# Retention with chunk products on halves of the tensor engine, one state sum per chunk, and a decay table from eight scans

## The chip, the cores and the metric

The kernel runs on one core of a Trainium2 chip. The metric is the device time of one execution in microseconds; lower is better. Times are medians of several executions; profiles come from one profiled execution.

## The reference

Three layers follow one another. Only the first, a retention (linear attention with a decay per head), is touched:

```python
# q, k, v: [B=2, H=8, S=768, D=64]; lam: [8]; block = 64
rel = pos[:, None] - pos[None, :]
Dmask = np.where(rel >= 0, lam[:, None, None] ** rel[None, :, :], 0.0)
lam_pow = lam[:, None, None] ** (pos[None, :, None] + 1)
lam_block = lam ** block
for b in range(nb):
    qb, kb, vb = q[:, :, sl], k[:, :, sl], v[:, :, sl]
    intra = np.einsum('bhic,bhjc->bhij', qb, kb) * Dmask[None]
    intra = np.einsum('bhij,bhjd->bhid', intra, vb)
    inter = np.einsum('bhid,bhde->bhie', qb * lam_pow[None], kv_state)
    out[:, :, sl] = intra + inter
    rev_pow = lam[:, None, None] ** (block - 1 - pos[None, :, None])
    kv_state = lam_block * kv_state + np.einsum('bhsd,bhse->bhde', kb * rev_pow, vb)
```

The result is the same for any block length. Behind it stand a layer norm with a two-layer network (512 to 2048 to 512, ReLU, residual) on 1,536 tokens, and an attention of four experts (64 wide) of which the two best by a gate are summed for each token.

## The kernel before

The retention runs over 12 chunks of 128 tokens (2 batches of 6), each with its own loads of `qkT` and `kv` (three buffers each). Inside a chunk it works with blocks of C = 64 tokens: the partitions hold two of them, LATE (partitions 0 to 63, since keys and values are stored backwards) and EARLY. All products of the retention are 64x64 in fp32 on a quarter of TensorE's array; each appears in the profile as two matmul passes with a weight load each.

For chunk n the loop at L647 does this:

- `ret_scores(n + 1)` (L328): 16 products of keys and queries into `sck`.
- `ret_state(n)` (L358): 16 products of decayed keys `kd` and values, one 64x64 state per head and block, into the other half of the same PSUM tile.
- `ret_inner(n)` (L391): 16 products of values and the decayed scores `a`, into a PSUM tile `po`.
- `ret_sum(n, EARLY)` (L370): VectorE adds the first block's state to the carried one (`st`, L379); it also waits for the inner products. GpSimd multiplies it by the decay of 64 tokens (`old`, L389).
- `ret_decay(n + 1)` (L346): decayed keys `kd` for three heads on ScalarE (L351) and five on GpSimd (L352), scores times decay table `a` on VectorE (L355).
- Steps of the layer norm of finished blocks of 384 tokens (`ln_a` to `ln_d`), as they come due.
- `room(early)`: side work on VectorE and ScalarE, taken from a list by costs in us until the room is used up. The list holds the norm's pieces and the decoding of the first weights of the network (`prep_parts`, 6 pieces for each of 4 weights in front of the end of the retention).
- `ret_sum(n, LATE)`: the second block's state sum, and `old` again.
- From chunk 5 on, if one is ready, one step of the network's first layer (`g1`, L504, 12 matmuls of 128x384); before chunk 5 three matmuls on zeros (`warm`).
- `ret_outer(n)` (L406): up to 16 products of states and scaled queries `qd`, added into `po`; `ret_qd(n + 1)` on GpSimd (L340).
- `leave()`, VectorE's and ScalarE's end of the expert step; `ret_copy(n)`: ScalarE copies `po` to `xT` (L423); a second `room`.

Two PSUM tiles of two banks (`ps_big`) carry `sck` and `po` in turn. The order on every engine's queue is the order of the program, written by hand. Only between the start (`begin`, closed at L290) and L637 does a planner place what stands on VectorE, ScalarE, GpSimd and the DMA queue.

At the start the decay table `dec` (128 x 8 x 64) comes from one scan over 512 elements on VectorE (L284), which needs two prepared tables: `mul` (lam, zero at the start of each head) and `one` (from `hit`, made by GpSimd). GpSimd makes the powers `qpow` by doubling (L298) and all constants of later layers (L303 to L315), and issues the load of `g_ln`.

After the last chunk the steps of the network follow (L691, then `mlp_step`).

Of the kernel before, what the change touches and what calls it, by code (L numbers as in the profile page):

```python
# [17 lines left out]
P = 128  # L18
# [11 lines left out]
C = 64  # L30
# [6 lines left out]

ROOM = ((0.7, 0.9), (1.4, 1.6))
# [31 lines left out]
def model(ctx, tc, qkT, kv, lam, g_ln, w12, wat, out):  # L70
# [191 lines left out]
    qpow = rc.tile([P, HP, C], F32, tag="qpow", name="qpow")  # L262
    lq = rc.tile([P, H], F32, tag="lq", name="lq")
    dec = rc.tile([P, H, C], F32, tag="dec", name="dec")
    mul = rc.tile([P, H, C], F32, tag="mul", name="mul")
    one = rc.tile([P, H, C], F32, tag="one", name="one")
    hit = rc.tile([P, C], F32, tag="hit", name="hit")
    order = [(b, c) for b in range(B) for c in range(NC)]
    begin = ExitStack()
    begin.enter_context(tc.manual_schedule(engines={  # L270
        mybir.EngineType.SP, mybir.EngineType.DVE, mybir.EngineType.Activation, mybir.EngineType.Pool}))
    nc.sync.dma_start(lq, lam.rearrange("h o -> o h").to_broadcast([P, H]))
    ret_load(*order[0])
    table = const.tile([P, 1], F32, tag="table", name="table")
# [44 lines left out]

    LATE, EARLY = 0, 1
    SCK, ST = {}, {}

    def half(a2):
        return ts(a2 * C, (a2 + 1) * C)

    def ret_scores(n):  # L328

# [676 lines left out]
```

## Time and profile before

| | us |
|---|---|
| median of 3 runs | 489.55 (487.71 to 490.32) |
| the profiled execution | 488.7 |
| its span, first to last instruction | 486.8 |
| TensorE matmul busy | 465.2 (96%), 4,219 instructions |
| VectorE busy | 337.4 (69%) |
| ScalarE busy | 198.0 (41%) |
| GpSimd busy | 99.4 (20%) |
| mean granted clock of TensorE | 0.993 |

The page gives busy time by engine, 40 slices of the span with the busy share of each engine, the granted clock and the DMA, the chain that ended last, and the costliest groups. PE is the matmul side of TensorE and PEld its weight loads, DVE is VectorE, ACT ScalarE, POOL GpSimd, SP the engine that issues most DMAs. PE's busy time counts a matmul from its start to its modelled end, so passes overlap: distances between starts tell more than durations. A wait stands with the engine that waited, the line it then ran, and what released it ("issue": nothing that the profile shows).

### The profile page before, as it was taken

Reading aid. Unit: us, or ns where it says so; the run is one execution under the profiler, and the core shown is the slowest. Engines: PE = TensorE matmul, PEld = TensorE weight load, DVE = VectorE, ACT = ScalarE, POOL = GpSimd, SP = SyncE. Lnnn points to the kernel's source line nnn. Section 1 sums busy time; section 2 is a strip of 40 time slices with the busy share of each in tenths; the row PEclk is TensorE's granted clock in tenths of the full one; section 3 lists DMA queues with packets and bytes.
Section 4 is the critical chain, followed back from the end, with each engine's and each line's share of the span. In section 5 each row is a group of like instructions: output and inputs, shape, how many; then the busy total and the mean of one; then the engine's idle time right before and its main releaser. Section 6 shows DMA issues by size and latency. Waiting matters only on the chain.

```text
span 486.8 us, 10377 instructions
## 1 busy us (share of the span) xinstructions
PE 465.2 (96%) x4219; PEld 432.4 (89%) x4224; DVE 337.4 (69%) x715; ACT 198.0 (41%) x453; POOL 99.4 (20%) x149
## 2 busy tenths in 40 slices
PE   7577989999999999999999999999999999999996
PEld 4456767999999999999999999999998889898884
DVE  2658795797999976942899935255478686676663
ACT  2337645532224331311233502122256666548672
POOL 6566452000000000000000000000045534334340
PEclk9979999999999999999999999999999999999999
DMA  8768520121232312210222400000000000000111
GB/s 286 298 205 294 179 92 3 43 88 44 87 131 86 114 60 88 87 44 1 86 88 86 131 0 2 0 1 1 0 2 0 24 23 22 24 3 23 44 43 67
DMA packets 10735, 35.28 MB, mean 72 GB/s; under 512 B 1344, under 2 KB 1600, under 8 KB 10688
## 3 DMA queue, kind: packets, MB, share of 16 engines
q1 hardware_dynamic: 10512, 34.49, 20.5%
q8 instruction: 33, 0.54, 0.5%
q10 hardware_dynamic: 144, 0.13, 0.1%
q14 instruction: 14, 0.11, 0.1%
q0 software_dynamic: 32, 0.00, 0.0%
HBM read 31.47 MB, written 3.15 MB: 71 GB/s over the span
## 4 chain that ended last, share of the span: by engine, by line
PE 84%; DVE 7%; ACT 3%; issue 3%; POOL 1%; DMA 1%; DVEq 0%; POOLq 0%; ACTq 0%
PE h L513 26%; PE y L547 26%; PE pj L764 4%; PE s L844 4%; PE av L893 4%; PE o L914 4%; PE t L881 4%; PE pv L786 3%; PE yf L566 2%; PE po L416 2%; PE sck L366 1%; PE po L399 1%; PE sck L336 1%; ACT xn L455 1%; PE warmc L106 1%
## 5 line engine op out<-in xcount | busy, mean ns | idle before, releaser
L513 PE MATMUL h<-xn,w 128*128 128x384 f32 x768 | 140.5, 337 | 0.0
L513 PEld LDWEIGHTS h<-xn,w 128*128 128x128 f32 x768 | 133.3, 188 | 2.7 <-issue 1.2
L547 PE MATMUL y<-hs,w 128*128 128x384 f32 x552 | 99.8, 334 | 0.0
L547 PEld LDWEIGHTS y<-hs,w 128*128 128x128 f32 x552 | 96.1, 188 | 0.0
L778 POOL TENSOR_SCALAR kh<-kh 64x384 fp32r<-64x384 f32 x16 | 8.4, 523 | 291.4 <-DVE qs L772 280.0
L532 ACT ACTIVATE hs<-h 128x384 fp32r<-128x384 f32 x50 | 24.5, 490 | 103.5 <-PE h L513 90.0
L533 DVE SCALAR_TENSOR_TENSOR hs<-h,hs 128x384 fp32r<-128x384 f32 x50 | 27.7, 555 | 42.5 <-ACT hs L532 42.5
L552 DVE TENSOR_TENSOR xT<-xT,y 128x768 f32<-128x768 f32 x30 | 28.5, 950 | 31.6 <-PE y L547 31.6
L871 POOL TENSOR_SCALAR att<-att,c,gw 128x128 f32<-128x128 f32 (+5 forms) x48 | 35.8, 752 | 52.0 <-DVE c L868 16.3
L231 ACT CAST w<-top 128x512 fp32r<-128x512 f32 x32 | 19.9, 621 | 48.0 <-DVE top L225 46.3
L764 PE MATMUL pj<-x,wa 128*128 128x384 f32 x192 | 35.0, 337 | 0.0
L764 PEld LDWEIGHTS pj<-x,wa 128*128 128x128 f32 x192 | 33.4, 188 | 0.0
L882 ACT COPY aT<-t 128x512 f32<-128x512 f32 (+3 forms) x64 | 26.6, 441 | 11.0 <-PE t L881 10.6
L881 PE MATMUL t<-ident,att 128*128 128x128 f32 x168 | 26.2, 275 | 0.3 <-DVE qs L772 0.3
L243 DVE TENSOR_TENSOR w<-top,mag 128x512 fp32r<-128x512 f32 x32 | 24.3, 758 | 0.3
L216 ACT ACTIVATE mag<-raw 128x512 f32<-128x512 f32 x32 | 21.2, 668 | 7.0 <-DVE w L243 7.0
L236 DVE SCALAR_TENSOR_TENSOR mag<-raw,mag 128x512 f32<-128x512 uint32 x32 | 23.3, 727 | 0.6
L893 PE MATMUL av<-aT,v 128*64 128x128 f32 x336 | 23.6, 280 | 0.0
L844 PE MATMUL s<-kh,qs 128*128 128x512 f32 (+3 forms) x64 | 23.3, 365 | 0.0
L225 DVE SCALAR_TENSOR_TENSOR top<-raw,mag 128x512 int32<-128x512 int32 x32 | 22.1, 689 | 0.5
L240 DVE TENSOR_TENSOR top<-top,w 128x512 f32<-128x512 f32 x32 | 22.4, 699 | 0.0
L893 PEld LDWEIGHTS av<-aT,v 128*64 128x64 f32 x336 | 17.8, 136 | 4.4 <-issue 3.9
(132 smaller groups left out, 735.9 us busy)
## 6 DMA issues: line engine op xcount, KB each, us to landing
raw<-in_w SPq DMA_DIRECT2D x32, 512.0 KB, 3.5
qk<-in_qkT SPq DMA_DIRECT2D x12, 512.0 KB, 5.2
kvn<-in_kv SPq DMA_DIRECT2D x12, 512.0 KB, 6.0
out<-os SPq DMA_DIRECT2D x11, 256.0 KB, 2.0
rawa<-in_wat SPq DMA_DIRECT2D x3, 512.0 KB, 3.2
rawa<-in_wat SPq DMA_DIRECT2D x1, 520.0 KB, 3.9
out<-os SPq DMA_DIRECT2D x1, 128.0 KB, 1.7
out<-os ACTq DMA_DIRECT2D x1, 128.0 KB, 1.7
```

The lines of the kernel that those rows point to most:

```text
L243: nc.vector.tensor_tensor(t["w"][:, 1], t["top"], t["mag"], ALU.add)
L513: nc.tensor.matmul(ph[:, :TB], w[:, wi, k, :], xn[:, xi, k, :], start=(i == 0), stop=(i == 11))
L532: LAST.append((nc.scalar.activation(h[:, 0], ph[:, :TB], AF.Relu), nc.vector.scalar_tensor_tensor(h[:, 1], ph[:, :TB], 0.0, h[:, 0].bitcas ...
L533: nc.vector.scalar_tensor_tensor(h[:, 1], ph[:, :TB], 0.0, h[:, 0].bitcast(F32), ALU.max, ALU.subtract)))
L547: nc.tensor.matmul(y[:, j, :TB], w[:, wi, e * P:(e + 1) * P], h[:, xi], start=(f == 0 and i == 0), stop=(f == GF - 1 and i == 2))
L552: nc.vector.tensor_tensor(xv, xv, y[:, :, :TB], ALU.add)
L764: nc.tensor.matmul(ps[:, :TB], w[:, wi, k, :], x2[:, xi, k, :], start=(i == 0), stop=(i == 11))
L844: nc.tensor.matmul(ps[:, c0:c1], q, kk[:, e, c0:c1], start=(i == 0), stop=(i == 1))
L871: nc.gpsimd.tensor_scalar(a[:, :n], a[:, :n], c, gw, ALU.mult, ALU.mult)
L881: nc.tensor.transpose(pt[:, (j - j0) * P:(j - j0 + 1) * P], a[:, j * P:(j + 1) * P], ident)
L882: nc.scalar.copy(aT[:, j0 * P:j1 * P], pt[:, :(j1 - j0) * P])
L893: nc.tensor.matmul(pav[e2 * HD:(e2 + 1) * HD, pr * P:(pr + 1) * P], v[:, j, e * HD:(e + 1) * HD], row["aT"][e][:, j * P:(j + 1) * P], star ...
```

## The change

The block becomes the chunk: 128 tokens. Scores are 8 products with 64 rows and 128 columns of the array and 128 moving columns; the state is one per head and chunk, 8 products over 128 rows; inner products are 8 over 128 rows with 128 moving columns; the cross-chunk products are 8 of 64x64 with 128 moving columns, and none in a batch's first chunk. One state sum and one `old` remain for each chunk, without the wait for the inner products, and none in a batch's last chunk (`old` not in the last two). State and output share one `po` tile, `sck` holds scores alone. The order in a chunk is scores(n + 1), state, cross-chunk, inner; then decay(n + 1), sum, `qd`(n + 1), copy; then norm steps, the network's step or `warm`, one `room` of 1.5 us (3.0 with a step), and the step's `leave`.

`dec` is 128 x 8 x 128 and comes from eight scans of 128 elements that read lam as a broadcast column, so `one` and `mul` go. `qpow` doubles once more. The constants of later layers are issued on GpSimd behind chunk 0's decayed keys, `g_ln` is loaded through ScalarE's queue ahead of its table load, and the whole start is in the order of the program. Of the products' functions (L322 to L423) the diff below shows the new form alone.

```diff
-ROOM = ((0.7, 0.9), (1.4, 1.6))
+ROOM = (1.5, 3.0)
...
-    qpow = rc.tile([P, HP, C], F32, tag="qpow", name="qpow")
+    qpow = rc.tile([P, HP, P], F32, tag="qpow", name="qpow")
     lq = rc.tile([P, H], F32, tag="lq", name="lq")
-    dec = rc.tile([P, H, C], F32, tag="dec", name="dec")
-    mul = rc.tile([P, H, C], F32, tag="mul", name="mul")
-    one = rc.tile([P, H, C], F32, tag="one", name="one")
-    hit = rc.tile([P, C], F32, tag="hit", name="hit")
+    dec = rc.tile([P, H, P], F32, tag="dec", name="dec")
+    hit = rc.tile([P, P], F32, tag="hit", name="hit")
     order = [(b, c) for b in range(B) for c in range(NC)]
-    begin = ExitStack()
-    begin.enter_context(tc.manual_schedule(engines={
+    by_hand = ExitStack()
+    by_hand.enter_context(tc.manual_schedule(engines={
         mybir.EngineType.SP, mybir.EngineType.DVE, mybir.EngineType.Activation, mybir.EngineType.Pool}))
     nc.sync.dma_start(lq, lam.rearrange("h o -> o h").to_broadcast([P, H]))
     ret_load(*order[0])
+    g_sb = const.tile([P, KT], F32, tag="g", name="g_sb")
+    nc.scalar.dma_start(g_sb, g_ln)
     table = const.tile([P, 1], F32, tag="table", name="table")
     nc.scalar.copy(table, zeros[:, :1])
     nc.gpsimd.memset(hit, 0.0)
-    for a2 in range(2):
-        nc.gpsimd.affine_select(hit, hit, [[1, C]], ALU.not_equal, 1.0, base=1 - C * (a2 + 1), channel_multiplier=1)
-    nc.vector.tensor_copy(one, hit[:, None, :].to_broadcast([P, H, C]))
-    nc.vector.tensor_copy(mul, lq[:, :, None].to_broadcast([P, H, C]))
-    nc.vector.memset(mul[:, :, 0:1], 0.0)
-    nc.vector.tensor_tensor_scan(dec.rearrange("p h i -> p (h i)"), mul.rearrange("p h i -> p (h i)"),
-                                 one.rearrange("p h i -> p (h i)"), 0.0, ALU.mult, ALU.add)
+    nc.gpsimd.affine_select(hit, hit, [[1, P]], ALU.not_equal, 1.0, base=1 - P, channel_multiplier=1)
+    for h in range(H):
+        nc.vector.tensor_tensor_scan(dec[:, h, :], lq[:, h:h + 1].to_broadcast([P, P]), hit, 0.0, ALU.mult, ALU.add)
     ret_load(*order[1])
     load_next()
     ret_load(*order[2])
     load_next(2)
-    begin.close()
-    g_sb = const.tile([P, KT], F32, tag="g", name="g_sb")
-    nc.gpsimd.dma_start(g_sb, g_ln)
     for h2 in range(2):
         nc.gpsimd.tensor_copy(qpow[h2 * D:(h2 + 1) * D, :, 0:1], lq[h2 * D:(h2 + 1) * D, h2 * HP:(h2 + 1) * HP, None])
     m = 1
-    while m < C:
+    while m < P:
         nc.gpsimd.tensor_tensor(qpow[:, :, m:2 * m], qpow[:, :, :m],
                                 qpow[:, :, m - 1:m].to_broadcast([P, HP, m]), ALU.mult)
         m *= 2
     sum_w = const.tile([P, 32], F32, tag="sumw", name="sum_w")
-    nc.gpsimd.memset(sum_w, 1.0 / DM)
     part_w = const.tile([P, P], F32, tag="partw", name="part_w")
-    nc.gpsimd.memset(part_w, 1.0 / 32)
     eps_sb = const.tile([P, 1], F32, tag="eps", name="eps_sb")
-    nc.gpsimd.memset(eps_sb, LN_EPS)
     ident = const.tile([P, P], F32, tag="ident", name="ident")
-    make_identity(nc, ident)
     tri = const.tile([P, P], I32, tag="tri", name="tri")
     fill = const.tile([P, P], F32, tag="fill", name="fill")
-    nc.gpsimd.memset(fill, 0.0)
-    nc.gpsimd.affine_select(fill, fill, [[-1, P]], ALU.is_ge, 1.0, base=0, channel_multiplier=1)
-    nc.gpsimd.tensor_copy(tri, fill)
-    nc.gpsimd.memset(fill, MASKED)
+    def constants():
+        nc.gpsimd.memset(sum_w, 1.0 / DM)
+        nc.gpsimd.memset(part_w, 1.0 / 32)
+        nc.gpsimd.memset(eps_sb, LN_EPS)
+        make_identity(nc, ident)
+        nc.gpsimd.memset(fill, 0.0)
+        nc.gpsimd.affine_select(fill, fill, [[-1, P]], ALU.is_ge, 1.0, base=0, channel_multiplier=1)
+        nc.gpsimd.tensor_copy(tri, fill)
+        nc.gpsimd.memset(fill, MASKED)
...
+    ST = {}
+    HEADS = [(hp, h2) for hp in range(HP) for h2 in range(2)]
+    def half(h2):
+        return ts(h2 * D, (h2 + 1) * D)
+    def cols(hp, n=P):
+        return ts(hp * n, (hp + 1) * n)
     def ret_scores(n):
+        r = R[order[n]]
+        sc = r["sc"] = ps_big(f"sc{n}")
+        for hp, h2 in HEADS:
+            nc.tensor.matmul(sc[:, h2, cols(hp)], r["qk"][half(h2), 1, hp, :], r["qk"][half(h2), 0, hp, :],
+                             start=True, stop=True)
+    def ret_qd(n):
+        b, c = order[n]
+        if c > 0:
+            r = R[b, c]
+            r["qd"] = r2.tile([P, HP, P], F32, tag="qd", name=f"qd{n}")
+            nc.gpsimd.tensor_tensor(r["qd"], r["qk"][:, 0], qpow, ALU.mult)
+    def ret_decay(n):
         b, c = order[n]
         r = R[b, c]
+        if c < NC - 1:
+            kvn = r["kvn"]
+            kd = r["kd"] = r2.tile([P, H, D], F32, tag="kd", name=f"kd{n}")
+            for h in range(3):
+                nc.scalar.mul(kd[:, h, :], kvn[:, 0, h, :], dec[:, h, P - 1:P])
+            nc.gpsimd.tensor_tensor(kd[:, 3:, :], kvn[:, 0, 3:, :],
+                                    dec[:, 3:, P - 1:P].to_broadcast([P, H - 3, D]), ALU.mult)
+        a = r["a"] = r2.tile([P, 2, HP, P], F32, tag="a", name=f"a{n}")
+        nc.vector.tensor_mul(a, r["sc"].rearrange("p h (k i) -> p h k i", k=HP),
+                             dec.rearrange("p (h k) i -> p h k i", h=2))
+    def ret_state(n):
         b, c = order[n]
+        r = R[b, c]
+        po = r["po"] = ps_big(f"po{n}")
+        if c < NC - 1:
+            for hp, h2 in HEADS:
+                nc.tensor.matmul(po[half(h2), 1, cols(hp, D)], r["kd"][:, h2 * HP + hp, :],
+                                 r["kvn"][:, 1, h2 * HP + hp, :], start=True, stop=True, skip_group_check=True)
+    def ret_outer(n):
+        b, c = order[n]
+        r = R[b, c]
+        if c > 0:
+            st = ST.pop(n - 1)
+            for hp, h2 in HEADS:
+                nc.tensor.matmul(r["po"][half(h2), 0, cols(hp)], st[half(h2), hp, :], r["qd"][half(h2), hp, :],
+                                 start=(hp == 0), stop=False, skip_group_check=True)
     def ret_inner(n):
         b, c = order[n]
         r = R[b, c]
+        for hp, h2 in HEADS:
+            nc.tensor.matmul(r["po"][half(h2), 0, cols(hp)], r["kvn"][:, 1, h2 * HP + hp, :], r["a"][:, h2, hp, :],
+                             start=(c == 0), stop=True, skip_group_check=True)
+    def ret_sum(n):
         b, c = order[n]
+        if c == NC - 1:
+            return
+        st = ST[n] = r2.tile([P, HP, D], F32, tag="st", name=f"st{n}")
+        pv = R[b, c]["po"][:, 1, :HP * D].rearrange("p (h e) -> p h e", h=HP)
+        if c == 0:
+            nc.vector.tensor_copy(st, pv)
+        else:
+            nc.vector.tensor_tensor(st, pv, ST["old"], ALU.add)
+        if c < NC - 2:
+            ST["old"] = r2.tile([P, HP, D], F32, tag="old", name=f"old{n}", bufs=1)
+            nc.gpsimd.tensor_tensor(ST["old"], st, qpow[:, :, P - 1:P].to_broadcast([P, HP, D]), ALU.mult)
+    def ret_copy(n):
+        b, c = order[n]
+        r = R.pop((b, c))
         t0 = b * S + c * P
+        nc.scalar.copy(xT[:, :, t0:t0 + P], r["po"][:, 0].rearrange("p (k i) -> p k i", k=KT))
...
-    SCK[0] = ps_big("sck0")
     ret_scores(0)
     warm(WARM[1], "b")
-    ret_decay(*order[0])
-    ret_qd(*order[0])
+    ret_decay(0)
+    constants()
     norm_at, n = [0] * NBLK, 0
     while n < len(order) or min(norm_at) < 4 or norm_parts or weight_parts:
         if n < len(order):
             if n + 3 < len(order):
                 ret_load(*order[n + 3])
-            SCK[n + 1] = ps_big(f"sck{n + 1}")
-            if n > 0:
+            if n + 1 < len(order):
                 ret_scores(n + 1)
             ret_state(n)
+            ret_outer(n)
             ret_inner(n)
-            if n == 0:
-                ret_scores(n + 1)
-            ret_sum(n, EARLY)
             if n + 1 < len(order):
-                ret_decay(*order[n + 1])
+                ret_decay(n + 1)
+            ret_sum(n)
+            if n + 1 < len(order):
+                ret_qd(n + 1)
+            ret_copy(n)
...
-            leave, early = None, ROOM[0]
-            if n >= MLP_FROM and any(ready(k, True) for k in range(len(FIRST) - len(steps) + len(todo))):
-                early = ROOM[1]
+            leave = next_step(True) if n >= MLP_FROM else None
+            if n < MLP_FROM:
+                warm(3, f"c{n}")
             if n > 0:
-                room(early[0])
-            ret_sum(n, LATE)
-            if early is ROOM[1]:
-                leave = next_step(True)
-            elif n < MLP_FROM:
-                warm(3, f"c{n}")
-            ret_outer(n)
-            if n + 1 < len(order):
-                ret_qd(*order[n + 1])
+                room(ROOM[leave is not None])
             if leave:
                 leave()
-            ret_copy(n)
-            if n > 0:
-                room(early[1])
```

## Rows read from the trace of the kernel before

**Rows 1.** Windows: busy us (xcount) of PE, PEld, DVE, ACT, POOL; then clock, DMA share, GB/s.

```profile
0.00:10.00 10.00, 7.33 (x75) 3.36 (x79) 3.16 (x6) 2.90 (x8) 7.61 (x27) 1.00 0.76 264
...
0.00:82.00 82.00, 65.05 (x1623) 49.19 (x1632) 54.28 (x92) 38.70 (x89) 46.52 (x69) 0.96 0.57 201
...
82.00:372.00 290.00, 289.93 (x1726) 287.65 (x1724) 207.16 (x399) 89.52 (x180) 8.68 (x16) 1.00 0.16 53
```

**Rows 2.** Windows: from chunk 0's to chunk 6's cross-chunk products, and on to chunk 11's end.

```profile
13.35:45.51 32.16, 23.63 (x763) 17.77 (x766) 20.04 (x35) 14.07 (x35) 19.66 (x22) 0.89 0.72 253
45.51:81.23 35.72, 30.31 (x716) 25.75 (x716) 29.92 (x50) 20.92 (x45) 18.12 (x20) 1.00 0.35 122
sum 67.88, PE 53.94 PEld 43.52 DVE 49.96 ACT 34.99 POOL 37.77; mean PE 26.97 PEld 21.76 DVE 24.98 ACT 17.49 POOL 18.89
```

**Rows 3.** Timeline of PE around chunk 9: start, us, instructions, idle before.

```profile
62.16 0.69 PE L336 MATMUL sck<-qk 64*64 64x64 f32 x32 [1.40 <-issue]
62.65 0.68 PE L366 MATMUL sck<-kvn,kd 64*64 64x64 f32 x32
63.11 0.68 PE L399 MATMUL po<-a,kvn 64*64 64x64 f32 x32
63.72 0.85 PE L433 MATMUL va<-dq,sum_w 128*32 128x384 f32 x8
...
67.43 1.15 PE L416 MATMUL po<-qd,st 64*64 64x64 f32 x32
```

**Rows 4.** Timeline of PE in the attention at the end (tiles of 128x64).

```profile
380.10 0.66 PE L893 MATMUL av<-aT,v 128*64 128x128 f32 x8
```

**Rows 5.** Waits of PE, 13 to 82 us: total us, times, longest.

```profile
PE sck L366 <- issue: 7.5, 5, 2.4
PE sck L336 <- issue: 1.4, 1, 1.4
PE sck L336 <- DVE st L379: 1.0, 1, 1.0
PE po L399 <- ACT xT L423: 0.9, 1, 0.9
PE sck L336 <- PE po L416: 0.8, 1, 0.8
PE po L416 <- DVE st L379: 0.7, 1, 0.7
PE sck L336 <- ACT xT L423: 0.7, 1, 0.7
```

**Rows 6.** Timeline of PE, 20 to 32.5 us: the longest stall, a product at half clock.

```profile
22.85 0.28 PE L366 MATMUL sck<-kvn,kd 64*64 64x64 f32 x3 [2.35 <-issue]
...
31.12 1.51 PE L433 MATMUL mu<-xT,sum_w 128*32 128x384 f32 x8
```

**Rows 7.** DMA by queue (packets, MB, share): stretches 0 to 82, then 20.3 to 23.

```profile
q8 instruction: 13, 0.21, 1.1%
...
q8 instruction: 1, 0.02, 2.5%
```

**Rows 8.** Groups by line (busy us, mean ns), to 82 us; then one of the page.

```profile
L355 DVE TENSOR_TENSOR a<-sck,dec 128x512 f32<-128x512 f32 x12 | 8.2, 681 | 0.1
...
L552 DVE TENSOR_TENSOR xT<-xT,y 128x768 f32<-128x768 f32 x30 | 28.5, 950 | 31.6 <-PE y L547 31.6
```

**Rows 9.** Timeline of the start: powers, decay scan, keys of chunks 0 and 1.

```profile
3.54 0.43 POOL L295 COPY qpow<-lq 64x4 f32<-64x4 f32 x2 [1.21 <-DMA lq<-in_lam]
...
5.70 1.22 DVE L284 TENSOR_TENSOR_SCAN dec<-mul,one 128x512 f32<-128x512 f32 x1
...
8.42 0.73 POOL L352 TENSOR_TENSOR kd<-kvn,dec 128x320 f32<-128x320 f32 x1
...
13.17 0.73 POOL L352 TENSOR_TENSOR kd<-kvn,dec 128x320 f32<-128x320 f32 x1
```

**Rows 10.** Windows right behind the retention.

```profile
sum 28.00, PE 28.00 PEld 26.24 DVE 22.70 ACT 13.09 POOL 0.00; mean PE 9.33 PEld 8.75 DVE 7.57 ACT 4.36 POOL 0.00
```

More of the change, by code (lines that the diff above doesn't have):

```diff
@@ L29 @@
 GF = 4
-C = 64
 H_BUFS = 5
@@ L313, in model @@
-    nc.gpsimd.affine_select(fill, fill, [[-1, P]], ALU.is_ge, 1.0, base=0, channel_multiplier=1)
-    nc.gpsimd.tensor_copy(tri, fill)
-    nc.gpsimd.memset(fill, MASKED)
-    xT = xpool.tile([P, KT, B * S], F32, tag="xT", name="xT")
[L322 to L326, printed above, removed]
-    def ret_scores(n):
-        if n < len(order):
-            r = R[order[n]]
-            qk, r["sc"] = r["qk"], SCK[n]
-            for hp in range(HP):
-                for h2 in range(2):
-                    for a2 in (LATE, EARLY):
-                        nc.tensor.matmul(r["sc"][half(a2), h2, hp * C:(hp + 1) * C], qk[half(h2), 1, hp, half(a2)],
-                                         qk[half(h2), 0, hp, half(1 - a2)], start=True, stop=True,
-                                         skip_group_check=True)
@@ L360, in ret_state @@
         r = R[b, c]
-        kvn, kd, ps = r["kvn"], r["kd"], SCK[n + 1]
-        halves = (EARLY,) if c == NC - 1 else (LATE, EARLY)
-        for hp in range(HP):
-            for h2 in range(2):
-                for a2 in halves:
-                    nc.tensor.matmul(ps[half(h2), a2, (HP + hp) * C:(HP + hp + 1) * C],
-                                     kd[half(a2), h2 * HP + hp, :], kvn[half(a2), 1, h2 * HP + hp, :],
-                                     start=True, stop=True, skip_group_check=True)
-    def ret_sum(n, a2):
-        b, c = order[n]
-        ps = SCK[n + 1]
-        if a2 == EARLY or c < NC - 1:
-            st = r2.tile([P, HP, D], F32, tag=f"st{a2}", name=f"st{b}{c}{a2}")
-            pv = ps[:, a2, HP * C:].rearrange("p (h e) -> p h e", h=HP)
-            if c == 0 and a2 == EARLY:
-                ins = nc.vector.tensor_copy(st, pv)
-            else:
-                ins = nc.vector.tensor_tensor(st, pv, ST["old"], ALU.add)
-            if a2 == EARLY:
-                for done in R[b, c]["inner"]:
-                    tc.add_manual_dep(ins.ins, done.ins.name, mybir.DependencyInfo(
-                        mybir.DependencyClass.Sync, mybir.DependencyReason.DATA), reason="rows")
-            ST[n, a2] = st
-            if c < NC - 1:
-                ST["old"] = r2.tile([P, HP, D], F32, tag="old", name=f"old{b}{c}{a2}")
-                nc.gpsimd.tensor_tensor(ST["old"], st, qpow[:, :, C - 1:C].to_broadcast([P, HP, D]), ALU.mult)
+        po = r["po"] = ps_big(f"po{n}")
[4 more added lines that the diff above has]
+    def ret_outer(n):
+        b, c = order[n]
+        r = R[b, c]
[4 more added lines that the diff above has]
+                                 start=(hp == 0), stop=False, skip_group_check=True)
     def ret_inner(n):
@@ L393, in ret_inner @@
         r = R[b, c]
-        po = r["po"] = ps_big(f"po{b}{c}")
-        r["inner"] = []
-        for hp in range(HP):
-            for h2 in range(2):
-                for a2 in (LATE, EARLY):
-                    mm = nc.tensor.matmul(
-                        po[half(h2), 1 - a2, hp * C:(hp + 1) * C], r["kvn"][half(a2), 1, h2 * HP + hp, :],
-                        r["a"][half(a2), h2, hp, :], start=(hp == 0), stop=(c == 0 and a2 == EARLY),
-                        skip_group_check=True)
-                    if hp == HP - 1:
-                        r["inner"].append(mm)
@@ L406, in ret_outer @@
-    def ret_outer(n):
-        b, c = order[n]
-        r = R[b, c]
-        po = r["po"]
-        for a2, st in ((LATE, ST.pop((n, EARLY))), (EARLY, ST.pop((n - 1, LATE), None))):
-            if st is None:
-                continue
-            for hp in range(HP):
-                for h2 in range(2):
-                    nc.tensor.matmul(po[half(h2), 1 - a2, hp * C:(hp + 1) * C], st[half(h2), hp, :],
-                                     r["qd"][half(h2), hp, 1 - a2, :], start=False, stop=True, skip_group_check=True)
+        for hp, h2 in HEADS:
+            nc.tensor.matmul(r["po"][half(h2), 0, cols(hp)], r["kvn"][:, 1, h2 * HP + hp, :], r["a"][:, h2, hp, :],
+                             start=(c == 0), stop=True, skip_group_check=True)
@@ L635, in next_step @@
         return None
-    by_hand = ExitStack()
-    by_hand.enter_context(tc.manual_schedule(engines={
-        mybir.EngineType.SP, mybir.EngineType.DVE, mybir.EngineType.Activation, mybir.EngineType.Pool}))
     del pieces[:len(first)]
-    SCK[0] = ps_big("sck0")
     ret_scores(0)
     warm(WARM[1], "b")
-    ret_decay(*order[0])
-    ret_qd(*order[0])
+    ret_decay(0)
+    constants()
     norm_at, n = [0] * NBLK, 0
```

18 lines of the change are left out of this document (removed).

## Prediction

> **What bounds the kernel now.** I read the windows first. From 82 to 372 us TensorE works 289.93 of 290.00 us at clock 1.00; before that it works 65.05 of 82.00 us at 0.96 [rows 1]. Since the change leaves everything behind the retention as it is, the end moves by as much as the moment from which TensorE no longer rests, about 82 us, where chunk 11's last product ends (81.23 us). Only the twelve chunks can gain or lose. From chunk 0's cross-chunk products (13.35 us) to that end they take 67.88 us: TensorE 53.94 us busy (0.79 of it), VectorE 49.96, GpSimd 37.77 [rows 2]. No engine is full, so this stage is bound by a chain in which the engines wait for each other. Its first half, six chunks, runs at clock 0.89. The waits of TensorE say what the rest is made of: 7.5 us in five stalls in the middle of the state products (L366) that no semaphore released ("issue"), and 5.5 us in six waits on VectorE's state sums, on ScalarE's copy and on what hangs on them, the last six rows there [rows 5].
>
> **What the change does to TensorE's array (term A).** Today each 64x64 product uses a quarter of the array and four run side by side: 16 products of scores are 32 passes, and from L336 to L366 to L399 the groups start 0.49 and 0.46 us apart [rows 3]. The cross-chunk products (L416) use two quarters: 1.15 us less the 0.2 us tail of the last pass, about 1.0. After the change scores, intra-chunk and cross-chunk products are 8 products = 16 passes on a half (cross-chunk: a quarter twice) with 128 moving columns. The nearest row is the attention's L893, 128x64 with 128 columns: 8 passes in 0.66 us, with a tail of 0.22, that is 55 ns a pass [rows 4]. So 16 passes take 0.88 us. Per chunk: scores +0.41, intra +0.41, cross-chunk -0.15, state the same (16 passes of half the length for 32 of today). Over the chunks behind the start: 11 x 0.41 + 11 x 0.41 - 10 x 0.15 is +7.5; the first chunks of both batches lose their half of the cross-chunk products and chunk 5 its state, together about -1.6. That is +5.9 us of array. It counts where TensorE is not waiting anyway, by its busy share 0.79: **+4.7** (between 0 and +5.9).
>
> **Changes of tile shape (term B).** Today the shape changes twice a chunk (quarters, whole array, quarters); afterwards scores, state, cross-chunk, intra and the 128x128 products all differ: five times. The row: between L399 and the mean's va the starts lie 0.61 us apart where 0.46 is the distance without a change, so a change costs 0.15 us [rows 3]. 3 x 0.15 x 10 chunks is 4.5; by the busy share **+3.6** (between 0 and +4.5). The Trainium skill, TensorEngine Tiling (Array Packing), Tiling Modes, says that changing the mode drains TensorE, which speaks against this change; it gives no price, and the 0.15 us of the row agrees that there is one.
>
> **Instruction stalls (term C).** In the first 82 us the instruction queue brings 13 packets for 1,623 matmuls and 1,632 weight loads; the longest stall, 2.35 us ending at 22.85 us, has exactly one such packet beside it [rows 1, 6, 7]. I take the five stalls as fetches that TensorE outran. The retention's passes fall from 1,472 (scores 384, state 352, intra 384, cross 352) to 704 (192, 160, 192, 160), and each has a weight load: 1,536 of 3,255 instructions go, 47%. Half of 7.5 us: **-3.7** (between 0, if the fewer crossings are all exposed, and -7.5, if passes of twice the length cover them). The Trainium skill, Runtime: NRT & Kernel Launch, Instruction fetch mechanics, says the opposite: crossing a block of instructions is mostly hidden. By it this term would be 0; the trace, with 7.5 us in which nothing else was late, does not agree so far.
>
> **Waits on sums and copies (term D).** A chunk has two state sums on VectorE today. The second stands behind the decode of expert weights, and the next scores wait for its PSUM tile: 1.0, 1.4 and 0.8 us [rows 5]. The copy to xT on ScalarE stands behind the leaving of an expert product (0.9 and 0.7), and the cross-chunk products wait 0.7 for the first sum. Afterwards there is one sum, ahead of that decode, the copy comes before the expert step, the scores' tile is freed by the decay product alone, and scores of the next chunk stand in front of whoever waits. **-5.5** (between 0 and -5.5). What is late next: the po tile has one buffer, so the state of n+1 waits for the copy of n; behind it on TensorE's queue stands all of chunk n+1. The next scores (0.88 us) cover it. VectorE's own work hardly changes: the decay product grows from 512 to 1024 elements, 0.681 us to about 1.22 (at the slope from it to the 768 elements of L552, 0.950), and one sum of 256 elements goes, about 0.41 by the same slope: +0.1 us a chunk, hidden under the 3.1 us of array that a chunk then has [rows 8]. GpSimd has one product of a chunk less.
>
> **Clock (term F).** Chunks 0 to 6 run at 0.89 [rows 2]; a mean product takes 1.51 us at half clock where the same shape takes 0.85 [rows 3, 6]. It fell behind stalls in the middle of products. Summed over the products of that stretch about 2.5 us; if most stalls go, **-2** (between 0 and -2.5).
>
> **The start (term G).** The decay table becomes 1024 elements of scan in eight pieces. The row has 1.22 us for 512 [rows 9]: 2.4 us without any cost of a piece, 3.4 with a fixed part of 0.14 us each (what the slope of rows 8 leaves of 0.681). But its input `hit` waits no longer behind GpSimd's other constants, and `one` and `mul` go, so it starts when lam lands (3.5 us) and not at 5.70: ready at 6 to 7 us, as now (6.92). Chunk 0's keys are at 8.42 on GpSimd and chunk 1's at 13.17, behind the first carried state [rows 9]. GpSimd's 7.61 us of work in the first 10 [rows 1] hold all that will stand ahead of chunk 1's keys, but for one doubling (256 elements, at most the 0.73 of 320 elements in chunk 0's keys). So these begin at about 10 to 11 us. **-2.5** (between 0, if the loads set the start, and -4). Moving the load of g to ScalarE's queue costs nothing visible: it stands before a table load, and the first keys come only at 7 us.
>
> **What is left behind (term H).** The room for side work is 1.5 or 3.0 us instead of two pieces of 0.7/0.9 or 1.4/1.6. Followed by the list's costs, one expert step fewer falls into the twelve chunks, and it comes back behind them: 0 in sum. Five VectorE instructions of the fourth weight, 512 elements each and so under the 0.950 us of L552's 768, move too: at most 4.7 us [rows 8]. Behind the retention VectorE works 22.70 of 28.00 us, 5.3 us are free [rows 10], and TensorE has one step more to do there. **+1** (between 0 and +3).
>
> **How the numbers follow.** 4.7 + 3.6 - 3.7 - 5.5 - 2 - 2.5 + 1 = -4.4 us. The profiled execution took 488.7 us (span 486.8 and 1.9 around it); 488.7 - 4.4 = **484.3 us**. It lies 0.85 us below the median of three runs, inside their spread, and I leave it so. A measurement of this kernel can tell about 0.5% from no change: faster is below 487.1, slower above 492.
>
> **The rivals.** *Forecast*, 480 to 488: 0.50, of which 0.07 end above 487.1. *All stalls go*: passes of twice the length cover every fetch, the clock stays up and the shape changes hide: 4.7 - 7.5 - 5.5 - 2.5 - 2.5 = -13.3, 475.4 us. For it: five stalls lie in the short state passes. Against: they would have to go to the last one. 0.12. *The fetches remain*: stalls of the same sum, on other products, and the clock with them: C and F are 0, the sum is +1.3, 490.0 us. The Trainium skill's rule named under C leaves C at 0 too. For it: thirteen packets make five stalls, so most are hidden already and the number may not matter. Against: the stalls come where instructions are shortest. 0.18, of which 0.05 above 492. *Slower: the copy of po becomes the wait.* Whoever waits for the copy today waits 0.8 us (0.9 and 0.7). With one po buffer the state of n+1, and all of TensorE behind it, waits for intra(n), then the copy; if ScalarE is late (four scalings and two squares of the norm stand on it) by more than the 0.88 us of scores, ten chunks pay 0.8: +8.0 in place of the -1.6 of D that copies gave, +9.6, sum +5.2, 493.9 us. It decides once more than half of the chunks wait. 0.20, of which 0.05 end below 492.
>
> Faster: 0.43 + 0.12 = 0.55. Same: 0.07 + 0.13 + 0.05 = 0.25. Slower: 0.05 + 0.15 = 0.20. The range leaves out the very end of the second case and, above, the sums of several bounds: 476 to 495.
>
> **What would show it.** Scores groups of 16 passes about 0.9 us apart (A); gaps of 0.15 us at each change of shape (B); six or seven packets in the instruction queue before the chunks end, and "issue" of about half of 7.5 us (C); no wait of scores for a sum (D); clock near 1.00 from 13 to 45 us (F); chunk 1's keys on GpSimd at 10 to 11 us (G); chunk 11's last product at about 75 us with one expert product more behind it, and VectorE over 0.85 busy there (H). I am wrong if TensorE waits for the copy in most chunks, or if the stalls keep their sum with half the instructions.

## The result and the profile after

| | before | after |
|---|---|---|
| median of 8 runs | 488.63 us (486.02 to 492.77) | 482.99 us (482.74 to 484.76) |
| ratio, 95% interval | | 0.9887 (0.9850 to 0.9924) |
| profiled execution, span | 488.7, 486.8 us | 484.76, 482.8 us |
| mean granted clock | 0.993 | 0.996 |

The change makes the kernel 1.1% faster, 5.5 us by the ratio (3.7 to 7.3); from profiled execution to profiled execution it is 3.9 us. The forecast was 4.4 less, 484.3 us. The profiled execution of after is the slowest of its eight (the other seven lie between 482.74 and 483.14, with the clock at 0.999 to 1.000); why, is seen below.

The windows of after, columns as in [rows 1]:

```profile
0.00:82.00 82.00, 75.83 (x879) 57.77 (x885) 57.34 (x85) 39.09 (x88) 32.64 (x52) 0.98 0.56 196
82.00:372.00 290.00, 289.46 (x1716) 287.49 (x1715) 210.65 (x407) 89.29 (x181) 10.24 (x19) 1.00 0.18 55
```

TensorE works 75.83 us of the first 82 where it was 65.05, and behind that it is full as before. The stage to look at is again the chunks. TensorE's timeline around chunks 9 to 11, in which the lines have become L326 (scores), L357 (state), L366 (cross-chunk), L373 (intra), L485 (expert step):

```profile
60.89 2.38 PE L485 MATMUL h<-xn,w 128*128 128x384 f32 x12
63.20 1.16 PE L326 MATMUL sc<-qk 64*128 64x128 f32 x16
64.30 0.69 PE L357 MATMUL po<-kvn,kd 128*64 128x64 f32 x16
64.91 1.09 PE L366 MATMUL po<-qd,st 64*64 64x128 f32 x16
65.93 1.09 PE L373 MATMUL po<-a,kvn 128*64 128x128 f32 x16
66.95 0.83 PE L456 MATMUL var<-part_w,vas 128*128 128x1 f32 x6
...
70.56 1.09 PE L366 MATMUL po<-qd,st 64*64 64x128 f32 x16
71.58 1.09 PE L373 MATMUL po<-a,kvn 128*64 128x128 f32 x16
72.60 2.36 PE L485 MATMUL h<-xn,w 128*128 128x384 f32 x12
```

No idle time is left in it. The kernel before, at chunk 11's cross-chunk products and at the first product of the second layer's main part, and the changed kernel at that product:

```profile
80.08 1.15 PE L416 MATMUL po<-qd,st 64*64 64x64 f32 x32
81.16 0.85 PE L433 MATMUL va<-dq,sum_w 128*32 128x384 f32 x8
...
118.32 2.35 PE L547 MATMUL y<-hw,w 128*128 128x384 f32 x12
```

```profile
114.42 2.35 PE L519 MATMUL y<-hw,w 128*128 128x384 f32 x12
```

Starts are now 1.10, 0.61, 1.02 and 1.02 us apart, 3.75 us for a full chunk; before it was 0.49, 0.46 and 0.61 [rows 3] and, for the cross-chunk products, 0.97 ahead of products of the same shape (chunk 10, 74.56 to 75.54 us) and 1.08 ahead of another shape (chunk 11): 2.53 to 2.64. What follows chunk 11's last product starts at 72.60 us instead of 81.16. Up to there three expert steps are done and not five, and two steps come back: the second layer's main part starts at 114.42 us against 118.32, and these 3.90 us are what arrives at the end.

The waits of TensorE from 13 to 82 us, and the instruction queue's packets in the first 82, where [rows 5] and [rows 7] had 7.5 us of stalls, 5.5 us of other waits and 13 packets:

```profile
PE sc L326 <- DMA qk<-in_qkT: 1.9, 1, 1.9
PE po L366 <- POOL qd L334: 1.4, 2, 0.8
PE warmc L104 <- issue: 0.5, 3, 0.2
```

```profile
q8 instruction: 7, 0.11, 0.5%
```

The stalls are gone, and so are all waits of scores on a sum. What is new is a wait for the loads of chunk 3. Of the 16 parts in which these queries land, 15 are there at 17.50 us and the last at 18.89; the first packet of instructions starts at 16.55 us, and from then on the last part of five loads in a row comes 1.4 us behind the others, where it came 0.1 to 0.2 behind them. That the packet held up this part is likely, since the other traces have the same lag (1.0 to 1.5 us) soon after their first packet, but no run tests it. Behind the wait lies the one stretch at half clock that remained in this execution:

```profile
19.03 1.72 PE L326 MATMUL sc<-qk 64*128 64x128 f32 x16 [1.87 <-DMA qk<-in_qkT]
20.68 1.12 PE L357 MATMUL po<-kvn,kd 128*64 128x64 f32 x16
21.73 1.63 PE L366 MATMUL po<-qd,st 64*64 64x128 f32 x16
23.29 1.09 PE L373 MATMUL po<-a,kvn 128*64 128x128 f32 x16
```

Scores, state and cross-chunk products start 1.65, 1.05 and 1.56 us apart there instead of 1.10, 0.61 and 1.02: 1.5 us, about what this execution lies above the other seven (1.6 to 2.0).

### The profile page after: what moved, and what is told of

Its sections match the earlier page's. It is cut to its first block, busy times and chain, and to the rows that moved or that the text cites. A ratio compares the mean times of both kernels' runs of the same rounds, so it can differ in the third digit from the quotient of the medians.

```text
span 482.8 us, 8791 instructions
## 1 busy us (share of the span) xinstructions
PE 472.1 (98%) x3451; PEld 437.9 (91%) x3456; DVE 340.3 (70%) x707; ACT 196.1 (41%) x447; POOL 85.3 (18%) x132
## 4 chain that ended last, share of the span: by engine, by line
PE 85%; DVE 5%; issue 3%; DMA 3%; POOL 2%; ACT 1%; SPq 0%; POOLq 0%; DVEq 0%; ACTq 0%
PE h L485 27%; PE y L519 26%; PE pj L722 4%; PE s L802 4%; PE av L851 4%; PE o L872 4%; PE t L839 4%; PE pv L744 3%; PE yf L538 2%; DMA kvn<-in_kv 2%; PE po L373 1%; POOL qd L334 1%; PE sc L326 1%; PE po L366 1%; DMA qk<-in_qkT 1%
## 5 line engine op out<-in xcount | busy, mean ns | idle before, releaser
L485 PE MATMUL h<-xn,w 128*128 128x384 f32 x768 | 140.2, 336 | 0.0
L485 PEld LDWEIGHTS h<-xn,w 128*128 128x128 f32 x768 | 133.4, 188 | 2.8 <-issue 0.8
L241 DVE TENSOR_TENSOR w<-top,mag 128x512 fp32r<-128x512 f32 x32 | 21.9, 685 | 0.4
L851 PEld LDWEIGHTS av<-aT,v 128*64 128x64 f32 x336 | 17.8, 136 | 4.4 <-issue 3.9
```

Source lines behind the costliest of these rows:

```text
L485: nc.tensor.matmul(ph[:, :TB], w[:, wi, k, :], xn[:, xi, k, :], start=(i == 0), stop=(i == 11))
L851: nc.tensor.matmul(pav[e2 * HD:(e2 + 1) * HD, pr * P:(pr + 1) * P], v[:, j, e * HD:(e + 1) * HD], row["aT"][e][:, j * P:(j + 1) * P], star ...
```

## The experiments

Times of variants are compared with 482.99 us for the changed kernel, or as a ratio to runs of the kernel before on the same chip. The changed kernel's runs lie within 0.4 us of each other but for one, and those of five variants of it (more instructions, scores twice, state beside intra, constants first, loads) within 1.1; in two others (no zeros, together) one run lies 1.0 and 2.0 us above the next, at a mean clock of 0.995 and 0.996 where the fastest has 1.00. Runs of the kernel before on one chip, and those of every variant with long series of passes on quarters, spread over 4 to 7 us. The changed kernel itself was not run again beside the variants, so differences of about 1 us and less are the least certain; that the variant with the constants first came out at 483.04 speaks for the comparison.

**More instructions.** Scores on quarters with 128 moving columns, cross-chunk and intra products in two parts.

```diff
+            for a2 in range(2):
+                nc.tensor.matmul(sc[half(a2), h2, cols(hp)], r["qk"][half(h2), 1, hp, half(a2)],
+                                 r["qk"][half(h2), 0, hp, :], start=True, stop=True, skip_group_check=True)
 # cross-chunk and intra products: the same with columns hp * P + i * D, i in (0, 1)
```

> The changed kernel with the same array work in more instructions: scores as 16 products of 64x64 with 128 moving columns, cross-chunk and intra products each split into two of 64 moving columns (a chunk has 112 passes instead of 64; the kernel before had 128). Theory (instruction stalls were half of what the kernel before lost, and went because instructions were halved): 11 to 13 packets in the instruction queue before the chunks end instead of 7, 'issue' stalls of 3 to 6 us come back on TensorE, 486 to 489 us. Rival (the stalls went because the waits of sums and copies went, which let the fetch run ahead): 7 packets may rise but no stall over 0.5 us, 483 to 484 us.

484.48 us (483.91 to 484.96), +1.5. Its timeline, with one packet of instructions arriving from 30.1 us on, and the number of packets up to 82 us:

```profile
29.79 1.10 PE L327 MATMUL sc<-qk 64*64 64x128 f32 x32
30.83 0.69 PE L358 MATMUL po<-kvn,kd 128*64 128x64 f32 x16
31.44 1.20 PE L368 MATMUL po<-qd,st 64*64 64x64 f32 x32
32.57 1.20 PE L377 MATMUL po<-a,kvn 128*64 128x64 f32 x32
33.70 0.91 PE L422 MATMUL mean<-mus,part_w 128*128 128x384 f32 x2
```

```profile
q8 instruction: 11, 0.18, 1.0%
```

Eleven packets, and no stall: the groups follow at 1.04, 0.61, 1.13 and 1.13 us. These distances differ from the changed kernel's by 0.16 us a chunk, 1.8 us in eleven chunks, which is about the whole difference. So 112 passes a chunk and eleven packets, where the kernel before had 128 and 13, don't stall TensorE by their number alone; this part of the theory fell.

**Quarters, at the pace of the kernel before.** As above, and the scores with 64 moving columns, 64 passes a chunk.

```diff
+                for i in range(2):
+                    nc.tensor.matmul(sc[half(a2), h2, ts(hp * P + i * D, hp * P + i * D + D)],
+                                     r["qk"][half(h2), 1, hp, half(a2)], r["qk"][half(h2), 0, hp, half(i)],
+                                     start=True, stop=True, skip_group_check=True)
```

> The changed kernel with scores on quarters of the array and 64 moving columns (32 products, 64 passes a chunk at the pace of the kernel before, 14.7 ns a pass) and cross-chunk and intra products split in two as in the run with more instructions: 144 passes a chunk, more than the 128 of the kernel before, with the order and the side work of the changed kernel. Theory (TensorE outruns its instruction fetch where passes are shorter than about 20 ns and many): 13 or more packets and stalls of 2 to 6 us, 486 to 490. Rival (the stalls hang on the order of the kernel before or on its loads, not on the number or pace of instructions): no stall over 0.5 us, 483.5 to 485.5.

490.40 us (487.75 to 491.58), +7.4. Its timeline at the stalls, and the packets:

```profile
14.74 0.76 PE L328 MATMUL sc<-qk 64*64 64x64 f32 x32 [0.89 <-issue]
...
20.37 1.09 PE L328 MATMUL sc<-qk 64*64 64x64 f32 x52 [0.83 <-issue]
...
42.65 0.51 PE L360 MATMUL po<-kvn,kd 128*64 128x64 f32 x10 [0.95 <-issue]
...
47.06 0.34 PE L360 MATMUL po<-kvn,kd 128*64 128x64 f32 x4 [0.39 <-issue]
```

```profile
q8 instruction: 14, 0.23, 1.1%
```

The stalls are back: 0.89, 0.83, 0.95 and 0.39 us, inside groups of products, with the order, the sums and the side work of the changed kernel. Each of the four has one instruction packet that starts 2.3 to 2.6 us ahead of its end (near 12.4, 17.8, 40.3 and 44.7 us), as the longest stall before had [rows 6, 7]. The array explains up to 3.9 us of the 7.4 (groups 1.23, 1.13 and 1.13 us instead of 1.10, 1.02 and 1.02), the stalls 3.0 of it in the profiled run, which was the fastest of ten and lies 4.8 us above the changed kernel; why the other nine took 1.4 to 3.8 us longer still, no trace shows.

That these stalls are fetches can be counted. When they begin, TensorE has started 448, 703, 958, 1,468 and 1,980 instructions of the trace in the kernel before, and 447, 702, 1,979 and 2,235 here. But for some missing records these numbers lie whole multiples of 256 apart, and some 256 is what one packet holds: 33 packets brought the kernel before about 8,500 instructions, 8,443 of them matmuls and weight loads. The changed kernel's wait for chunk 3's queries begins at 293 and is no such place.

The 64 passes of the scores follow at 19 ns here, and the 32 of the run above at 32 ns, where nothing stalled. But a chunk also has 144 passes instead of 112: pace and number changed together, and no run tells them apart. An estimate speaks for the pace: a packet's 256 instructions are 128 passes, which would last 1.9 to 2.5 us at the 15 to 19 ns seen where TensorE stalls and 4.1 us at 32 ns, against 2.2 to 2.6 us from a packet's start to the end of its stall.

**Scores twice.**

```diff
+        for _ in range(2 if 0 < n else 1):
             for hp, h2 in HEADS: ...
```

> The changed kernel with the scores of chunks 1 to 11 computed twice into the same place: 11 x 16 passes x 55 ns = 9.7 us more of array work, nothing else. Theory (TensorE is the bound of the changed retention, so array work counts in full): 491 to 494 us. Rival (TensorE's share 0.79 as in the prediction, or less, if VectorE and the chain bind): 4 to 8 us more, 487 to 491 us.

489.08 us (488.56 to 489.52), +6.1. The scores' group takes 1.99 us from start to start, and the wait for loads is what became smaller:

```profile
24.11 2.06 PE L327 MATMUL sc<-qk 64*128 64x128 f32 x32
26.10 0.69 PE L358 MATMUL po<-kvn,kd 128*64 128x64 f32 x16
```

```profile
PE sc L327 <- DMA qk<-in_qkT: 2.3, 3, 1.1
```

0.89 us more in eleven chunks is 9.8 us of array; 6.1 arrive, 0.62. That is the rival's range, not the theory's: array work doesn't count in full. Of the 3.7 us that don't arrive, 2.0 are found in the waits that the changed kernel still has, for scaled queries (1.4 to none) and loads (2.9 to 2.3 over the first 82 us); the rest isn't assigned.

**State beside intra.**

```diff
-            ret_state(n)
             ret_outer(n)
+            ret_state(n)
             ret_inner(n)
```

> The changed kernel with the order cross-chunk, state, intra in place of state, cross-chunk, intra: state and intra have the same tile shape (128x64), so one change of shape of five goes in each of 9 chunks. Theory (a change costs 0.15 us, term B): scores to cross to state to intra is 0.1 to 0.15 us a chunk shorter, about 1 us less, 482. Rival (no price of a change of shape shows, or the state now waits for the scaled queries): 482.8 to 484.5.

483.91 us (483.81 to 484.17), +0.9. Cross-chunk, state and intra in this order, and the waits:

```profile
31.18 1.09 PE L367 MATMUL po<-qd,st 64*64 64x128 f32 x16 [0.28 <-POOL qd L334]
32.20 0.69 PE L357 MATMUL po<-kvn,kd 128*64 128x64 f32 x16
32.72 1.05 PE L374 MATMUL po<-a,kvn 128*64 128x128 f32 x16
33.69 0.91 PE L418 MATMUL mean<-mus,part_w 128*128 128x384 f32 x2
```

```profile
PE po L367 <- POOL qd L334: 5.1, 6, 1.4
```

Cross-chunk, state and intra products take 1.02, 0.52 and 0.97 us from start to start, 2.51 together; in the changed kernel state, cross-chunk and intra take 0.61, 1.02 and 1.02, 2.65. So one change of shape fewer is worth 0.14 us, 0.09 of it at the end of the state and 0.05 at the end of the intra products, about the 0.15 of term B. But the cross-chunk products came earlier by the state's time and wait 5.1 us for the scaled queries instead of 1.4: the order lost more than the shapes gave.

**Sum and copy first, in the kernel before.**

```diff
+            ret_sum(n, LATE)
             if n > 0:
                 room(early[0])
-            ret_sum(n, LATE)
...
+            ret_copy(n)
             if leave:
                 leave()
-            ret_copy(n)
```

> The kernel before with one part of the change alone: the second state sum stands ahead of the decode work, and the copy to xT ahead of the leaving of an expert product. Theory (waits on sums and copies cost 5.5 us, term D): 4 to 5 us less than before, 484 to 485 us, and no wait of scores for a sum. Rival (that time was covered by the instruction stalls or by VectorE's own work): within 1.5 us of before, 487 to 490 us.

490.59 us, ratio 1.0031 (0.9997 to 1.0066): no gain. Waits of TensorE:

```profile
PE sck L366 <- issue: 8.0, 4, 3.2
PE po L399 <- ACT xT L423: 5.4, 5, 2.2
PE sck L336 <- DVE mag L220: 0.4, 1, 0.4
PE sck L336 <- PE po L416: 0.4, 1, 0.4
```

The waits of scores fell from 3.9 us [rows 5] to 0.8, as meant. The intra products' wait for the copy rose from 0.9 to 5.4: a sum ahead lets TensorE arrive earlier at a `po` tile that ScalarE hasn't emptied, and the stalls are as long as ever.

**Sum and queries behind the room, in the changed kernel.**

```diff
-            ret_sum(n)
-            if n + 1 < len(order):
-                ret_qd(n + 1)
-            ret_copy(n)
...
                 room(ROOM[leave is not None])
+            ret_sum(n)
+            if n + 1 < len(order):
+                ret_qd(n + 1)
             if leave:
                 leave()
+            ret_copy(n)
```

> The changed kernel with its one state sum and the scaled queries put behind the decode work, and the copy behind the leaving of an expert product, where the kernel before had its second sum and its copy. Theory (term D belongs to the new structure: with one sum for a chunk and TensorE as the bound the places matter): TensorE waits for the queries in most chunks, 1 to 2 us in ten chunks, 488 to 496 us. Rival (the places are worth nothing, as in the kernel before): within 1.5 us of 483.0.

499.83 us, ratio to before 1.0239 (1.0188 to 1.0290), +16.8. The timeline of all engines near 30 us:

```profile
29.92 0.43 DVE L219 TENSOR_SCALAR mag<-mag 128x512 int32<-128x512 int32 x1
30.26 0.42 DVE L385 TENSOR_TENSOR st<-po,old 128x256 f32<-128x256 f32 x1
30.71 0.58 ACT L395 COPY xT<-po 128x512 f32<-128x512 f32 x1 [1.29 <-DVE st L385]
31.35 0.69 PE L357 MATMUL po<-kvn,kd 128*64 128x64 f32 x16 [1.20 <-ACT xT L395]
```

The sum starts when the decode is done, the copy when the sum is done, and the state of the next chunk, and with it all of TensorE, waits 1.20 us for the copy. The clock falls to 0.86 from 45 to 82 us. This is the rival of the prediction, the copy of `po` as the wait, made true by a place in the order. The changed kernel has the same chain, only early enough; its timeline:

```profile
15.30 1.09 PE L373 MATMUL po<-a,kvn 128*64 128x128 f32 x16
16.52 0.42 DVE L385 TENSOR_TENSOR st<-po,old 128x256 f32<-128x256 f32 x1 [1.56 <-PE po L373]
16.97 0.59 ACT L395 COPY xT<-po 128x512 f32<-128x512 f32 x1 [2.38 <-DVE st L385]
```

The sum reads only the state, which was done long before, yet it starts after the intra products, and the copy after the sum, as if both were ordered by the whole `po` tile; what orders them is not shown further. The text ahead of the prediction says that the sum no longer waits for the inner products; in the trace it does.

**The start alone, in the kernel before; constants first, in the changed kernel.**

```diff
 # kernel before: constants moved into a function behind the first keys; g on ScalarE's queue
     ret_decay(*order[0])
+    constants()
 # changed kernel
-    ret_decay(0)
     constants()
+    ret_decay(0)
```

> The kernel before with the start of the change alone (constants behind chunk 0's keys, g through ScalarE's queue, all by hand; the decay table still by one scan). Theory (term G): chunk 1's keys on GpSimd about 2 us earlier, time 2 us less, 486 to 487 us. Rival (the loads set the start, or the next stall takes it): 488 to 490 us, within 1 us of before.

486.97 us, ratio 0.9957 (0.9918 to 0.9995): 2.1 us less (0.2 to 4.0).

> The changed kernel with the constants on GpSimd ahead of chunk 0's decayed keys, where they end 2 us later. Theory (in the changed kernel the start is bound by loads: TensorE waits 0.8 us for chunk 1's queries and 1.9 us for chunk 3's): the delay is taken up by these waits, within 0.7 us of 483.0. Rival (term G: the keys set the start): 1.5 to 2.5 us more, 484.5 to 485.5.

483.04 us (482.80 to 483.18), the same as the changed kernel. There the keys of chunks 0 and 1 on GpSimd are at

```profile
7.36 0.73 POOL L344 TENSOR_TENSOR kd<-kvn,dec 128x320 f32<-128x320 f32 x1
...
9.93 0.73 POOL L344 TENSOR_TENSOR kd<-kvn,dec 128x320 f32<-128x320 f32 x1
```

and with the constants first chunk 0's come at 9.33, 2 us later. The time doesn't change: the scores of chunk 3 start at 19.02 us, as before at 19.03, when their queries have landed, and the wait there is 1.2 us instead of 1.9. The wait of 0.8 us for chunk 1's queries that the expectation names doesn't stand in the changed kernel's trace. In the kernel before an earlier start is worth something; in the changed one the loads take up a later place of the keys.

**Loads.** Two weights of 512 KB requested behind chunk 3's loads, in the changed kernel and in the one before:

```diff
     ret_load(*order[2])
-    load_next(2)
...
                 ret_load(*order[n + 3])
+                load_next(2 if n == 0 else 0)
```

> The changed kernel with the second and third expert weight requested behind chunk 3's loads instead of ahead of them (1 MB later). Theory (in the changed kernel the start is bound by loads: TensorE waits 1.9 us for chunk 3's queries): that wait goes, 1.5 to 2 us less, 481 to 481.5, clock 1.00 in the profile. Rival (chunk 3's own requests stand behind the buffers, not behind the weights): within 0.5 us of 483.0.

481.87 us (481.55 to 482.03), -1.1, less than the wait that went (1.9); a wait of 0.8 us for chunk 2's queries, ending at 12.50 us, has come in its place.

> The kernel before with the second and third expert weight requested behind chunk 3's loads. Theory (the instruction stalls are a matter of TensorE's pace, not of the traffic of loads): five stalls in the state products as before, together 6 to 8 us, 487 to 490. Rival (instruction packets are late because they stand behind loads): the stall that ends near 22.9 us shrinks by over 1 us and the time falls to 485 to 487.

488.44 us, ratio 1.0003 (0.9974 to 1.0031): nothing. The stalls keep their sum, in four instead of five:

```profile
PE sck L365 <- issue: 7.3, 4, 3.0
```

**No matmuls on zeros.**

```diff
-            if n < MLP_FROM:
-                warm(3, f"c{n}")
```

> The changed kernel without the three matmuls on zeros in chunks 0 to 4. They lie 0.75 us apart from what follows (5 x 0.75 = 3.7 us of array). Theory (TensorE is the bound; scores computed twice cost 0.63 of their array time): 2 to 3.5 us less than 483.0, so 479.5 to 481, clock still near 1.00. Rival (the clock needs them, or a load takes their place): clock below 0.99 or waits for loads grow by as much, 482.5 to 486.

482.59 us (482.35 to 483.86), -0.4. TensorE waits 6.3 us for loads of queries in the first 82 us instead of 2.9. The clock stays at 1.00, although the wait for chunk 3's queries, behind which the changed kernel's profiled execution fell to half clock, is 2.7 us here: the length of the wait alone doesn't make the clock fall.

**Together.** Loads later, no zeros, and the scaled queries of n + 1 ahead of the carried state of n on GpSimd:

```diff
                 ret_decay(n + 1)
+                ret_qd(n + 1)
             ret_sum(n)
-            if n + 1 < len(order):
-                ret_qd(n + 1)
             ret_copy(n)
```

> A version built from the runs: the changed kernel with the two weights requested behind chunk 3's loads, no matmuls on zeros inside the chunks, and on GpSimd the scaled queries of n+1 ahead of the carried state of n (they need no sum; TensorE waited 1.4 to 1.8 us for them). Theory (TensorE is the bound where loads allow): 1.1 from the loads, 0.4 to 2 from the zeros once loads come earlier, up to 1.4 from the queries: 479 to 481 us. Rival (chunk loads are the next bound and take all): 481.5 to 482.5.

478.63 us (478.27 to 481.53), ratio to before 0.9831 (0.9795 to 0.9867): 8.3 us less than before and 4.4 less than the changed kernel, faster than both. Its waits from 12 to 82 us:

```profile
PE sc L325 <- DVE a L346: 1.6, 1, 1.6
PE sc L325 <- DMA qk<-in_qkT: 1.4, 1, 1.4
PE po L356 <- ACT xT L394: 0.2, 1, 0.2
```

None for the scaled queries is left. The parts had given 1.1 and 0.4 by themselves; what the queries give alone wasn't run. A decay product behind decode work (1.6) and loads (1.4) are next.

## Why the prediction was right

The time (482.99 for 484.3) and the sign are right, and so is the frame: only the chunks move, and the end of the kernel moves with them (3.90 us at the second layer, 3.9 at the end). That TensorE becomes nearly full there, 75.83 of 82 us, the prediction didn't say; it went on counting array work at a share of 0.79. That the sum came out is in part luck: term C was 3.8 us too small, and term D counted 5.5 us that no run shows as a gain of its own, so the time is no proof of each term.

- **Array and shapes (A, B).** Forecast 0.67 and 0.45 us a full chunk, together 1.12; measured 1.1 to 1.2 (3.75 less 2.53 to 2.64). A change of shape costs 0.14 us by the run with state beside intra, forecast 0.15, so B is right and the passes themselves (A) cost about 0.8. The Trainium skill's statement that a change of tiling mode drains TensorE (TensorEngine Tiling (Array Packing), Tiling Modes) agrees, at that price. The exposed share was taken as 0.79; scores twice gives 0.62, so about 6.5 us instead of 8.3.
- **Instruction stalls (C).** Forecast -3.7, half of them; all 7.5 us went. The step that failed is the reason: "half the instructions, half the stalls". With eleven packets no stall returned; with more and faster passes they did. The other bound that I had named, passes of twice the length cover the fetch, is the one that came; that the pace and not the number does it is likely by the estimate above, but not shown apart. The Trainium skill's rule that crossing a block of instructions is mostly hidden (Runtime: NRT & Kernel Launch, Instruction fetch mechanics) holds for the changed kernel and for the run with more instructions, and doesn't hold for long series of passes on quarters.
- **Waits on sums and copies (D).** Forecast -5.5, from adding up waits of the trace. As a term of its own it is not there: the same places in the kernel before gave nothing (ratio 1.0031), since the copy's wait and the stalls took them over; the old places in the changed kernel cost 16.8 us. (The wait of 1.4 us that [rows 5] puts down to "issue" was rightly counted here: it is gone with the sum ahead.) It is a condition of the new structure, not a gain to add. Adding waits counted time that other waits stood behind.
- **Clock (F).** Forecast -2: the profiled execution still has one stretch at half clock, the other seven, by their mean clock of 0.999 to 1.000, have next to none, and 1.6 to 2.0 us lie between.
- **Start (G).** Forecast -2.5; alone in the kernel before 2.1 (0.2 to 4.0). Chunk 1's keys at 9.93, forecast 10 to 11. What I did not see is that the next thing late are chunk 3's loads, which take 1.9 us back in the profiled execution.
- **Left behind (H).** Forecast +1 and one expert step fewer. Three stand ahead of chunk 11's end instead of five (a fourth is right behind it), and VectorE has room for it: behind the chunks, in 27.40 us, TensorE rests for none and VectorE is busy 0.87 of it:

```profile
sum 27.40, PE 27.40 PEld 24.88 DVE 23.76 ACT 15.68 POOL 0.00; mean PE 9.13 PEld 8.29 DVE 7.92 ACT 5.23 POOL 0.00
```

- **The slower rival** did not come, but its mechanism is real (sum behind the room); the forecast named the scores (0.88 us, measured 1.10) as the cover, and without the zeros, when least stands beside them, TensorE waits for the copy only once, 0.2 us.

What stays open: why the fetch starts so late in some places. A stall ends 2.2 to 2.6 us after its packet starts, and sometimes TensorE had over a hundred instructions left at that moment, sometimes none. Two loads fewer ahead of it change nothing (488.44). Pace and number of passes are not told apart. And the gain is not divided exactly: 8.6 us at the end of the chunks less two expert steps of 2.36 make 3.8, about the 3.9 that arrive, but no run takes the stalls alone out of the kernel before.

## What to carry to other kernels

Count passes of small products by their pace as well as by their array time: halves of the array with twice the moving columns cost 1.1 to 1.2 us more a chunk here and were still the faster form, in a kernel in which the stalls on instruction fetch (7.5 us) and the waits on sums and copies (5.5 us) went with them. Don't add up waits of one trace as gains: a wait that is removed uncovers the one behind it, and only an experiment on the part alone tells how much arrives. Where one engine has become full, look at once for what it still waits for; here three small moves in order gave another 4.4 us.

## What the runs showed of the hardware

- Kernels with series of 64 to 96 passes on quarters, 15 to 19 ns apart, stall at some of the places where a new packet of 256 instructions begins, for 0.4 to 3.2 us; with passes 32 ns apart and longer no run here stalled, with 11 packets in 82 us.
- Kernels with these stalls spread by 4 to 7 us between runs (490.40: 487.75 to 491.58), those without mostly by about 1 us or less (489.08: 488.56 to 489.52); the sum behind the room, with a low clock, is an exception (497.35 to 500.90).
- From the first instruction packet on, the last of the 16 parts of a load comes 1.0 to 1.5 us behind the others for several loads in a row (1.4 in the changed kernel, from 16.55 us on).
- One change of tile shape costs about 0.14 us (2.65 to 2.51 us for the same three groups); the changed kernel's one execution with a stretch at half clock took 1.6 to 2.0 us more than the others.
